# Decay table moved to the loads' queue, activation table first, and zero matmuls in the waits of the first three chunks

## The chip, the cores and the metric

The kernel runs on one core of a Trainium2 chip. The metric is the device time of one execution in microseconds (us). TensorE (PE) multiplies matrices and loads their stationary operand on a side path (PEld); VectorE (DVE), ScalarE (ACT) and GpSimd (POOL) work on elements; SyncE (SP) and ACT issue DMA transfers here, each on a queue of its own, and all transfers run on the core's 16 DMA engines. An engine takes its instructions in the order in which they stand in its program, and so does a queue.

## The reference

Three stages follow one another: attention with a decay, a gated MLP, and a second MLP with `h * cos(h)`. Only the first stage is touched by the change. Its core:

```python
for b in range(nb):                      # blocks of 64 positions
    qb, kb, vb = (q[:, :, sl], k[:, :, sl], v[:, :, sl])
    intra = np.einsum('bhic,bhjc->bhij', qb, kb) * Dmask[None]     # lam ** (i - j), 0 above the diagonal
    intra = np.einsum('bhij,bhjd->bhid', intra, vb)
    inter = np.einsum('bhid,bhde->bhie', qb * lam_pow[None], kv_state)
    out[:, :, sl] = intra + inter
    kb_dec = kb * rev_pow[None]
    kv_state = lam_block[None, :, None, None] * kv_state + np.einsum('bhsd,bhse->bhde', kb_dec, vb)
```

There are 2 batches, 8 heads, 768 positions and a head size of 64; the MLPs take 1536 tokens of 512, with inner sizes 1536 and 2048, weights in float64.

## The kernel before

The attention runs in 12 chunks of 128 positions (6 in each batch), all 8 heads at once, two heads side by side on the 128 partitions. For chunk g the steps are, each a function:

- `load_qkv` (L215) issues the loads of q, k and v, 256 KB each, on SP's queue, into 3, 3 and 5 buffers.
- `att_t` (L275) has TensorE transpose q (with `anti`, which also reverses it) and k (with `ident`), and ScalarE copy the results to `qt` and `kt` (L279).
- `att_scores` (L331) multiplies `kt` and `qt`; `att_mask` (L337) has VectorE multiply the scores with the decay table `dmask`, giving `at`.
- `att_kd` (L293) has GpSimd scale k with a column of `dmask`; `att_state` (L308) multiplies `kd` and v into the running state.
- `att_out` (L351, and L357 for the state's part) gives the chunk's output, which ScalarE and VectorE split into a high and a low half (L93, L94).

`dmask` (512 KB) is built at the start. `lam` is loaded, VectorE works out its powers in `down` (seven steps, L240), ScalarE's queue writes `down` to DRAM as `down_d` (L245, 8 KB), and reads it back with an overlapping access pattern into all partitions (L247). The read has to wait until the write has landed; both are instructions in ScalarE's program, and what stands behind them on ScalarE waits too. Behind them stand the load of the activation table (with a one-column `warm` activation, L511) and then the copies of `qt` and `kt`. `spread` (L255) brings the row of powers to all partitions with a small matmul (`lrow`).

The order of everything is written out by hand: `manual_schedule` records the program in the order in which the functions are called. The start of it is

```python
tables()                       # lam, q0 k0 q1 k1, powers, down_d, dmask, v0, q2 k2
load_qkv(1, "v"); load_qkv(3, "qk"); load_qkv(2, "v")
for _ in range(WARM):          # WARM = 10 matmuls of zeros, 512 columns, bf16
    nc.tensor.matmul(ps, zeros[:, 0:P], zeros, start=True, stop=True)
att_t(0); att_scores(0); spread()
att_t(1, "acc"); att_scores(1)
att_mask(0); att_kd(0); att_mask(1); att_kd(1)
```

and then a loop over g: `att_state(g)`, `att_kd(g + 2)`, `att_out(g)`, for g = 0 also `att_t(2)`, the loads of chunk g + 4 (v of g + 3), in most turns one 512 KB piece of MLP weights on SP's queue, `att_scores(g + 2)`, `att_mask(g + 2)`, `att_t(g + 3)`. From g = 6 on, the first matmuls of the gated MLP are mixed in; after the attention the MLPs run with TensorE busy nearly without a gap.

The load of k of chunk 3 takes the buffer of k of chunk 0, and so waits on SP's queue for `att_kd(0)`, which needs `dmask`.

Of the kernel before, what the change touches and what calls it, by code (L numbers as in the profile page):

```python
# [12 lines left out]
AF = mybir.ActivationFunctionType  # L13
# [19 lines left out]
WARM = 10  # L33
# [4 lines left out]
def kernel(  # L38
# [17 lines left out]
    nc = tc.nc  # L56
    B, H, S, D = q.shape
    P = 128
# [3 lines left out]
    C = P  # L62
# [24 lines left out]
    def bank(where):  # L87
        pool = ps_acc if where == "acc" else ps_mm
        return pool.tile([P, 512], F32, tag=where, name=where)
# [118 lines left out]
    def load_qkv(g, what="qkv"):  # L208
        if g >= NCH:
            return  # L210
        for nm in what:
            b, c = divmod(g, CPB)
            src, bufs = {"q": (q, 3), "k": (k, 3), "v": (v, 5)}[nm]
            t = att.tile([P, H, D], F32, tag=nm, name=nm, bufs=bufs)
            nc.sync.dma_start(t, src[b, :, c * C:(c + 1) * C, :].rearrange("h p d -> p h d"))  # L215
            qkv[g, nm] = t
# [5 lines left out]
    down = att.tile([H, 2 * C], F32, name="down", bufs=1)  # L222
    anti = att.tile([P, P], F32, name="anti", bufs=1)
    dmask = att.tile([P, H, C], F32, name="dmask", bufs=1)
    sel = att.tile([H, DM], F32, name="sel", bufs=1)
    lrow = att.tile([P, NPAIR, C], F32, name="lrow", bufs=1)
    state = [att.tile([P, NPAIR, P], F32, name=f"state{i}", bufs=1) for i in range(2)]

    def tables():

        nc.scalar.dma_start(down[:, C - 1:C], lam.rearrange("(h o) -> h o", o=1))
        load_qkv(0, "qk")
        load_qkv(1, "qk")
        nc.vector.memset(down[:, C + 1:], 0.0)
        nc.vector.memset(down[:, C:C + 1], 1.0)
        n = 1
        while n < C:
            nc.vector.tensor_scalar(  # L240
                out=down[:, C - 2 * n:C - n], in0=down[:, C - n:C],
                scalar1=down[:, C - n:C - n + 1], scalar2=None, op0=ALU.mult,
            )
            n *= 2
        nc.scalar.dma_start(down_d, down)  # L245
        e = down_d[:, :]
        nc.scalar.dma_start(dmask, bass.AP(e.tensor, e.offset + 1, [[1, P], [2 * C, H], [1, C]]))  # L247
        load_qkv(0, "v")
        load_qkv(2, "qk")

    def spread():

        ps = bank("acc")
        for p in range(NPAIR):
            nc.tensor.matmul(  # L255
                ps[:, p * C:(p + 1) * C], sel[:, p * P:(p + 1) * P], down[:, 0:C],
                start=True, stop=True,
            )
        nc.vector.tensor_copy(lrow.rearrange("p a i -> p (a i)"), ps)
# [7 lines left out]
            xs[nm, blk] = tuple(xp.tile([P, KD, TB], F32R, tag=t, name=t) for t in ("xh", "xl"))  # L267
        return xs[nm, blk]

    def att_t(g, where="mm"):  # L270

        for nm, src, perm in (("qt", qkv[g, "q"], anti), ("kt", qkv[g, "k"], ident)):
            ps = bank(where)
            for p in range(NPAIR):
                nc.tensor.transpose(  # L275
                    ps[:, p * P:(p + 1) * P], src[:, 2 * p:2 * p + 2, :].rearrange("p a d -> p (a d)"), perm
                )
            t = att.tile([P, NPAIR, C], F32, tag=nm, name=nm)
            nc.scalar.activation(t.rearrange("p a i -> p (a i)"), ps, AF.Copy)  # L279
            live[g, nm] = t  # L280
            if nm == "qt" and g % CPB:
                qd = att.tile([P, NPAIR, C], F32, tag="qd", name="qd", bufs=3)
                nc.vector.tensor_tensor(
                    out=qd[:, :, ::-1], in0=ps.rearrange("p (a i) -> p a i", a=NPAIR), in1=lrow, op=ALU.mult
                )
                live[g, "qd"] = qd
                tick()
# [33 lines left out]
                nc.vector.tensor_copy(new[r, :, r], pv[r])  # L321
        tick()

    def att_scores(g):
        qt, kt = live[g, "qt"], live[g, "kt"]
        got = live[g, "s"] = [bank("mm") for _ in range(2)]

        for p in range(NPAIR):
            for h2, ps in enumerate(got):
                r = slice(64 * h2, 64 * h2 + 64)  # L330
                nc.tensor.matmul(ps[:, p * C:(p + 1) * C], kt[r, p, :], qt[r, p, :], start=True, stop=True)  # L331
# [11 lines left out]
    def att_out(g):  # L343
        at, vn = live.pop((g, "at")), qkv[g, "v"]
        ps = bank("acc")
        inter = g % CPB != 0

        for p in range(NPAIR):
            cs = slice(p * C, (p + 1) * C)
            for h2 in range(2):  # L350
                nc.tensor.matmul(  # L351
                    ps[64 * h2:64 * h2 + 64, cs], vn[:, 2 * p + h2, :], at[:, 2 * p + h2, :],
                    start=p == 0, stop=not inter and p == NPAIR - 1, skip_group_check=True,
                )
        if inter:
            for p in range(NPAIR):
                nc.tensor.matmul(  # L357
                    ps[:, p * C:(p + 1) * C], state[g % 2][:, p, :], live[g, "qd"][:, p, :],
                    start=False, stop=p == NPAIR - 1, skip_group_check=True,
                )  # L360
        xh, xl = x_tiles(g // CB)
        o = (g % CB) * C
        split(xh[:, :, o:o + C], xl[:, :, o:o + C], ps.rearrange("p (a i) -> p a i", a=NPAIR))
# [129 lines left out]


    with tc.manual_schedule():
        nc.vector.memset(halfpi, math.pi / 2)
        zeros = att.tile([P, 512], mybir.dt.bfloat16, name="zeros", bufs=1)
        nc.vector.memset(zeros, 0.0)
        nc.gpsimd.memset(anti, 0.0)
        nc.gpsimd.affine_select(  # L500
            out=anti, in_=anti, compare_op=ALU.not_equal, fill=1.0, base=1 - P, pattern=[[1, P]], channel_multiplier=1
        )
        make_identity(nc, ident)
        nc.gpsimd.tensor_copy(
            sel.rearrange("k (h d) -> k h d", d=D), ident[0:H, 0:H].rearrange("k (h o) -> k h o", o=1).to_broadcast([H, H, D])
        )
        tables()
        load_qkv(1, "v")
        load_qkv(3, "qk")
        load_qkv(2, "v")  # L510
        nc.scalar.activation(warm, halfpi, AF.Silu)  # L511
        for t in state:
            nc.vector.memset(t, 0.0)

        ps = bank("acc")
        for _ in range(WARM):
            nc.tensor.matmul(ps, zeros[:, 0:P], zeros, start=True, stop=True)
        att_t(0)
        att_scores(0)
        spread()  # L520
        att_t(1, "acc")
        att_scores(1)
        att_mask(0)
        att_kd(0)
        att_mask(1)
        att_kd(1)
        for g in range(NCH):
            chunk[0] = g
            att_state(g)
            if g + 2 < NCH:  # L530
                att_kd(g + 2)
            att_out(g)
            if g == 0:
                att_t(2, "acc")
            load_qkv(g + 4, "qk")
            load_qkv(g + 3, "v")
            for _ in range(RAWS[g]):
                if n_loaded[0] - n_conv[0] + len(converting) < STAGE:
                    load_piece()
            if g + 2 < NCH:  # L540
                att_scores(g + 2)
                att_mask(g + 2)
            if g + 3 < NCH:
                att_t(g + 3)
            half = HALVES.index(g) if g in HALVES else -1
            if half >= 0:
                (produce_val if half % 2 else produce_gate)(half // 2, "acc")
                if half % 2:
                    finish(half // 2)()
        while converting:  # L550
            tick(age=0)
        flush()
        while n_loaded[0] - n_conv[0] < STAGE:
            load_piece()
        att_stack.close()
        mlp["sum"] = ctx.enter_context(tc.tile_pool(name="sum", bufs=NBLK))
        ring.append(ctx.enter_context(tc.tile_pool(name="ring_b", bufs=RING_B)))
        done = 0
        finished = len(HALVES) // 2
        convert(finished - 1, 0)  # L560
        for u in range(finished, NU):
            ph = units[u][0]
            low = []

            def finish_to(n):
                nonlocal finished
                while finished <= n:
                    low.append(finish(finished))
                    finished += 1

            produce(u)
            finish_to(u - ph)
            while done <= u - LAG:
                consume(done)
                done += 1
            convert(u, (2 if u < EASE else 1) if units[u][0] == 0 else u % 2)
            for fn in low:
                fn()
        while finished < NU:
            finish(finished)()  # L580
            finished += 1
        while done < NU:
            consume(done)
            done += 1
# [30 lines left out]
```

## Time and profile before

| | |
|---|---|
| Median of 3 runs | 632.95 us (631.49, 633.10, 632.95) |
| The profiled execution's own time | 632.53 us |
| Its span, first to last instruction | 630.5 us |
| PE busy | 619.2 us, 98% of the span |
| PE's share of the chain that ended last | 96% |
| ACT and DVE in that chain | 1% each |
| Mean granted TensorE clock | 0.989 of full |

The profile gives, for each engine, how long it was busy, in total and in slices of the span; the granted clock of TensorE; for each instruction its start, its length and what ended the engine's idle time before it; and the chain of work followed back from the last instruction. The time of an execution is longer than its span by what lies around it, here 632.53 − 630.5 = 2.03 us.

### The profile page before, as it was taken

To read this page: it belongs to the slowest core of one execution; us is meant where nothing else is said; L and a number is where in the kernel's file an instruction comes from. 1 tells how busy PE (TensorE), PEld (TensorE's weight loads), DVE (VectorE), ACT (ScalarE), POOL (GpSimd) and SP (SyncE) were. 2 spreads that over 40 slices of the span, in tenths; PEclk is the share of its full clock that TensorE was granted. 3 is DMA by queue.
4 is the path that set the end of the run, shared out by engine and by line. 5 is a ranking of instruction groups with operands and counts; after the bars stand their busy time and mean duration, and the time that the engine had idled before them with its cause. 6 is when DMAs were issued, how large, how long until landed. Compare 5 with 4: busy or idle time off the path is not lost.

```text
span 630.5 us, 8212 instructions
## 1 busy us (share of the span) xinstructions
PE 619.2 (98%) x3186; PEld 512.3 (81%) x3186; DVE 417.9 (66%) x632; ACT 272.0 (43%) x462; POOL 133.0 (21%) x115
## 2 busy tenths in 40 slices
PE   6999999999999999999999999999999999999997
PEld 4788888888888888888888888888888888888886
DVE  2677746778887613487514788897788678766655
ACT  1334334554334311334213465555555555544441
POOL 2224411333333200023203434101101010100000
PEclk7799999999999999999999999999999999999999
DMA  9998223444434200235200120212121110000103
GB/s 184 182 232 232 75 66 103 134 133 135 133 101 151 83 1 0 68 111 155 67 1 33 35 67 34 68 33 68 33 68 34 68 33 2 0 2 1 67 4 131
DMA packets 65431, 49.30 MB, mean 78 GB/s; under 512 B 38760, under 2 KB 60272, under 8 KB 65392
## 3 DMA queue, kind: packets, MB, share of 16 engines
q1 hardware_dynamic: 64320, 48.24, 27.1%
q10 hardware_dynamic: 1072, 0.53, 0.4%
q8 instruction: 25, 0.41, 0.3%
q14 instruction: 14, 0.11, 0.1%
HBM read 45.61 MB, written 3.15 MB: 77 GB/s over the span
## 4 chain that ended last, share of the span: by engine, by line
PE 96%; DVE 1%; ACT 1%; DMA 1%; issue 0%; ACTq 0%
PE mm L99 16%; PE mm L100 16%; PE mm L101 16%; PE acc L99 13%; PE acc L101 13%; PE acc L100 13%; PE mm L331 2%; PE acc L351 2%; PE acc L357 2%; PE mm L275 1%; PE acc L308 1%; DMA down_d<-down 1%; DVE sum L471 0%; PE acc L275 0%; ACT kt L279 0%; PE acc L255 0%
## 5 line engine op out<-in xcount | busy, mean ns | idle before, releaser
L99 PE MATMUL mm<-xl,wh 128*128 128x512 f32 x456 | 177.4, 389 | 0.0
L100 PE MATMUL mm<-xh,wl 128*128 128x512 f32 x456 | 177.4, 389 | 0.0
L101 PE MATMUL mm<-xh,wh 128*128 128x512 f32 x456 | 177.4, 389 | 0.0
L94 POOL TENSOR_TENSOR wl<-cw,wh 128x512 fp32r<-128x512 f32 x68 | 93.1, 1380 | 372.1 <-ACT wh L93 339.8
L433 DVE TENSOR_TENSOR g<-s,mm 128x512 f32<-128x512 f32 x81 | 55.4, 683 | 77.8 <-PE mm L101 75.5
L101 PEld LDWEIGHTS mm<-xh,wh 128*128 128x128 f32 x456 | 85.6, 188 | 17.8
L100 PEld LDWEIGHTS mm<-xh,wl 128*128 128x128 f32 x456 | 85.6, 188 | 17.7
L99 PEld LDWEIGHTS mm<-xl,wh 128*128 128x128 f32 x456 | 85.6, 188 | 17.7
L438 DVE TENSOR_TENSOR gl<-g,gh 128x512 fp32r<-128x512 f32 x84 | 68.1, 811 | 30.4 <-ACT gh L434 30.4
L434 ACT ACTIVATE gh<-g 128x512 fp32r<-128x512 f32 x84 | 52.3, 623 | 73.1 <-DVE g L433 73.1
L99 PE MATMUL acc<-wl,gh 128*128 128x512 f32 x192 | 74.7, 389 | 0.0
L100 PE MATMUL acc<-wh,gl 128*128 128x512 f32 x192 | 74.7, 389 | 0.0
L101 PE MATMUL acc<-wh,gh 128*128 128x512 f32 x192 | 74.7, 389 | 0.0
L144 ACT ACTIVATE ct<-raw 128x512 f32<-128x512 f32 x68 | 45.5, 670 | 65.6 <-DVE cw L161 38.3
L424 ACT ACTIVATE s<-s 128x512 f32<-128x512 f32 x48 | 30.4, 633 | 77.4 <-DVE s L423 77.4
L159 DVE TENSOR_SCALAR cw<-raw 128x512 int32<-128x512 int32 x68 | 49.5, 728 | 21.4 <-POOL wl L94 21.3
L422 DVE SCALAR_TENSOR_TENSOR s<-n,mm 128x512 f32<-128x512 int32 x48 | 32.9, 685 | 37.9 <-ACT n L421 37.7
L99 PE MATMUL acc<-gl,wh 128*128 128x512 f32 x144 | 56.0, 389 | 0.0
L100 PE MATMUL acc<-gh,wl 128*128 128x512 f32 x144 | 56.0, 389 | 0.0
L101 PE MATMUL acc<-gh,wh 128*128 128x512 f32 x144 | 56.0, 389 | 0.0
L161 DVE SCALAR_TENSOR_TENSOR cw<-ct,cw 128x512 int32<-128x512 int32 x68 | 49.0, 721 | 2.1
L165 DVE SCALAR_TENSOR_TENSOR cw<-raw,cw 128x512 int32<-128x512 int32 x68 | 48.0, 706 | 2.1
(75 smaller groups left out, 692.5 us busy)
## 6 DMA issues: line engine op xcount, KB each, us to landing
raw<-in_moe_w_out_dram SPq DMA_DIRECT2D x28, 512.0 KB, 3.3
raw<-in_moe_w_in_dram SPq DMA_DIRECT2D x16, 512.0 KB, 3.7
raw<-in_moe_w_gate_dram SPq DMA_DIRECT2D x12, 512.0 KB, 3.6
raw<-in_moe_w_val_dram SPq DMA_DIRECT2D x12, 512.0 KB, 3.7
q<-in_q_dram SPq DMA_DIRECT2D x12, 256.0 KB, 4.9
k<-in_k_dram SPq DMA_DIRECT2D x12, 256.0 KB, 4.8
v<-in_v_dram SPq DMA_DIRECT2D x12, 256.0 KB, 5.1
out_dram<-sum SPq DMA_DIRECT2D x12, 256.0 KB, 2.0
```

Of the source, the lines that this page charges most:

```text
L94: (sub or nc.vector).tensor_tensor(out=lo, in0=src, in1=hi.bitcast(F32), op=ALU.subtract)
L99: nc.tensor.matmul(ps, wh, xl, start=first, stop=False)
L100: nc.tensor.matmul(ps, wl, xh, start=False, stop=False)
L101: nc.tensor.matmul(ps, wh, xh, start=False, stop=last)
L144: nc.scalar.activation(t, words[:, :, 1].bitcast(F32), AF.Copy, scale=2.0 ** -112)
L159: nc.vector.tensor_scalar(out=w, in0=lo, scalar1=29, scalar2=None, op0=ALU.logical_shift_right)
L161: nc.vector.scalar_tensor_tensor(out=w, in0=t.bitcast(I32), scalar=3, in1=w, op0=ALU.logical_shift_left, op1=ALU.bitwise_or)
L165: nc.vector.scalar_tensor_tensor(out=w, in0=hi, scalar=-0x80000000, in1=w, op0=ALU.bitwise_and, op1=ALU.bitwise_or)
L422: nc.vector.scalar_tensor_tensor(out=s, in0=n_, scalar=-TWO_PI_1, in1=up, op0=ALU.mult, op1=ALU.add)
L433: nc.vector.tensor_tensor(out=g, in0=s, in1=up, op=ALU.mult)
L434: nc.scalar.activation(gh, g, AF.Copy)
L438: nc.vector.tensor_tensor(out=gl, in0=g, in1=gh.bitcast(F32), op=ALU.subtract)
```

## The change

The read of `dmask` moves from ScalarE's queue to SP's, behind the loads of q, k of chunks 0 and 1 and v of chunk 0, which in turn moves ahead of q and k of chunk 2. The activation table is loaded before the write of `down_d`. `spread` goes ahead of `att_scores(0)`. TensorE gets 15 more matmuls of zeros beside the ten that it had, each 512 columns in bf16: 2 ahead of `att_t(1)`, 4 ahead of `att_scores(1)`, 3 ahead of `att_out(0)`, 2 ahead of `att_t(2)` and 4 ahead of `att_scores(2)`. They write the PSUM bank that the step behind them then overwrites. The memset of `zeros` becomes VectorE's first instruction.

```diff
@@ -222,6 +222,7 @@
     down = att.tile([H, 2 * C], F32, name="down", bufs=1)
     anti = att.tile([P, P], F32, name="anti", bufs=1)
     dmask = att.tile([P, H, C], F32, name="dmask", bufs=1)
+    zeros = att.tile([P, 512], mybir.dt.bfloat16, name="zeros", bufs=1)
     sel = att.tile([H, DM], F32, name="sel", bufs=1)
     lrow = att.tile([P, NPAIR, C], F32, name="lrow", bufs=1)
     state = [att.tile([P, NPAIR, P], F32, name=f"state{i}", bufs=1) for i in range(2)]
@@ -231,8 +232,10 @@
 
 
         nc.scalar.dma_start(down[:, C - 1:C], lam.rearrange("(h o) -> h o", o=1))
+        nc.scalar.activation(warm, halfpi, AF.Silu)
         load_qkv(0, "qk")
         load_qkv(1, "qk")
+        load_qkv(0, "v")
         nc.vector.memset(down[:, C + 1:], 0.0)
         nc.vector.memset(down[:, C:C + 1], 1.0)
         n = 1
@@ -244,8 +247,7 @@
             n *= 2
         nc.scalar.dma_start(down_d, down)
         e = down_d[:, :]
-        nc.scalar.dma_start(dmask, bass.AP(e.tensor, e.offset + 1, [[1, P], [2 * C, H], [1, C]]))
-        load_qkv(0, "v")
+        nc.sync.dma_start(dmask, bass.AP(e.tensor, e.offset + 1, [[1, P], [2 * C, H], [1, C]]))
         load_qkv(2, "qk")
 
     def spread():
@@ -267,10 +269,16 @@
             xs[nm, blk] = tuple(xp.tile([P, KD, TB], F32R, tag=t, name=t) for t in ("xh", "xl"))
         return xs[nm, blk]
 
-    def att_t(g, where="mm"):
+    def zero(ps, n):
+        for _ in range(n):
+            nc.tensor.matmul(ps, zeros[:, 0:P], zeros, start=True, stop=True)
+
+    def att_t(g, where="mm", idle=0):
 
         for nm, src, perm in (("qt", qkv[g, "q"], anti), ("kt", qkv[g, "k"], ident)):
             ps = bank(where)
+            if nm == "qt":
+                zero(ps, idle)
             for p in range(NPAIR):
                 nc.tensor.transpose(
                     ps[:, p * P:(p + 1) * P], src[:, 2 * p:2 * p + 2, :].rearrange("p a d -> p (a d)"), perm
@@ -321,9 +329,10 @@
                 nc.vector.tensor_copy(new[r, :, r], pv[r])
         tick()
 
-    def att_scores(g):
+    def att_scores(g, idle=0):
         qt, kt = live[g, "qt"], live[g, "kt"]
         got = live[g, "s"] = [bank("mm") for _ in range(2)]
+        zero(got[0], idle)
 
         for p in range(NPAIR):
             for h2, ps in enumerate(got):
@@ -343,6 +352,8 @@
     def att_out(g):
         at, vn = live.pop((g, "at")), qkv[g, "v"]
         ps = bank("acc")
+        if g == 0:
+            zero(ps, 3)
         inter = g % CPB != 0
 
         for p in range(NPAIR):
@@ -493,9 +504,8 @@
 
 
     with tc.manual_schedule():
+        nc.vector.memset(zeros, 0.0)
         nc.vector.memset(halfpi, math.pi / 2)
-        zeros = att.tile([P, 512], mybir.dt.bfloat16, name="zeros", bufs=1)
-        nc.vector.memset(zeros, 0.0)
         nc.gpsimd.memset(anti, 0.0)
         nc.gpsimd.affine_select(
             out=anti, in_=anti, compare_op=ALU.not_equal, fill=1.0, base=1 - P, pattern=[[1, P]], channel_multiplier=1
@@ -508,18 +518,14 @@
         load_qkv(1, "v")
         load_qkv(3, "qk")
         load_qkv(2, "v")
-        nc.scalar.activation(warm, halfpi, AF.Silu)
         for t in state:
             nc.vector.memset(t, 0.0)
 
-        ps = bank("acc")
-        for _ in range(WARM):
-            nc.tensor.matmul(ps, zeros[:, 0:P], zeros, start=True, stop=True)
-        att_t(0)
+        att_t(0, idle=WARM)
+        spread()
         att_scores(0)
-        spread()
-        att_t(1, "acc")
-        att_scores(1)
+        att_t(1, "acc", idle=2)
+        att_scores(1, idle=4)
         att_mask(0)
         att_kd(0)
         att_mask(1)
@@ -531,14 +537,14 @@
                 att_kd(g + 2)
             att_out(g)
             if g == 0:
-                att_t(2, "acc")
+                att_t(2, "acc", idle=2)
             load_qkv(g + 4, "qk")
             load_qkv(g + 3, "v")
             for _ in range(RAWS[g]):
                 if n_loaded[0] - n_conv[0] + len(converting) < STAGE:
                     load_piece()
             if g + 2 < NCH:
-                att_scores(g + 2)
+                att_scores(g + 2, idle=0 if g else 4)
                 att_mask(g + 2)
             if g + 3 < NCH:
                 att_t(g + 3)
```

On SP's queue, at the start of the program (q, k, v are the chunks' loads, in the order q0 k0 q1 k1 v0, then `dmask`, then q2 k2 v1 q3; the names in brackets are semaphores that a row waits for):

```order
 L215 DMA k<-in_k_dram 128x8x64
 L215 DMA v<-in_v_dram 128x8x64
+L250 DMA dmask<-down_d 128x8x128 [waits DMAHW4_49]
 L215 DMA q<-in_q_dram 128x8x64 [waits DMAHW0_49]
 L215 DMA k<-in_k_dram 128x8x64 [waits DMAHW1_49]
 L215 DMA v<-in_v_dram 128x8x64 [waits DMAHW2_49]
```

The new row waits for the write of `down_d`, and the loads of chunk 2, v of chunk 1 and all later loads stand behind it.

On ScalarE, at the start of the program, before the change:

```order
L233 DMA down<-in_lam_dram 8x1
L245 DMA down_d<-down 8x256 [waits DMAHW0_49,DVE_49]
L247 DMA dmask<-down_d 128x8x128 [waits DMAHW4_49]
L511 ACT_TABLE_LOAD
L511 ACTIVATE warm<-halfpi 128x1
L279 ACTIVATE qt<-mm 128x512 [waits PE_49]
```

and after it:

```order
L234 DMA down<-in_lam_dram 8x1
L235 ACT_TABLE_LOAD
L235 ACTIVATE warm<-halfpi 128x1 [waits DVE_49]
L248 DMA down_d<-down 8x256 [waits DMAHW0_49,DVE_49]
L287 ACTIVATE qt<-mm 128x512 [waits PE_49]
```

Between the write of `down_d` and the first copy of `qt` nothing is left on ScalarE.

On TensorE, from the first transposes to the output of chunk 0, before the change:

```order
L275 MATMUL mm<-anti,q 128x128 x4
L275 MATMUL mm<-ident,k 128x128 x4
L331 MATMUL mm<-qt,kt 128x128 x8
L255 MATMUL acc<-down,sel 128x128 x4
L275 MATMUL acc<-anti,q 128x128 x4
L275 MATMUL acc<-ident,k 128x128 x4
```

and after it (a pair of rows with `zeros` is one matmul of zeros and its weights):

```order
L283 MATMUL mm<-ident,k 128x128 x4
L257 MATMUL acc<-down,sel 128x128 x4
L340 MATMUL mm<-qt,kt 128x128 x8
L274 LDWEIGHTS zeros
L274 MATMUL acc<-zeros 128x512
...
L283 MATMUL acc<-anti,q 128x128 x4
L283 MATMUL acc<-ident,k 128x128 x4
L274 LDWEIGHTS zeros
L274 MATMUL mm<-zeros 128x512
...
L340 MATMUL mm<-qt,kt 128x128 x8
L316 MATMUL acc<-v,kd 64x64 x8
```

The small matmul of `spread` now stands between the transposes and the scores of chunk 0, and zeros stand ahead of the steps of chunk 1.

## Rows read from the trace of the kernel before

**Rows 1.** Page, part 2: 40 equal slices, PE busy and granted clock in tenths.

```profile
PE   6999999999999999999999999999999999999997
PEclk7799999999999999999999999999999999999999
```

**Rows 2.** Windows: stretch, length, busy us (instructions) PE, PEld, DVE, ACT, POOL; PEclk, DMA share, GB/s.

```profile
4.00:6.00 2.00, 2.00 (x9) 1.08 (x8) 0.94 (x2) 0.00 (x0) 0.00 (x0) 1.00 1.25 219
...
8.00:10.00 2.00, 0.00 (x0) 0.00 (x0) 0.00 (x0) 1.81 (x3) 0.00 (x0) 0.71 1.35 218
...
20.00:22.00 2.00, 2.00 (x26) 1.79 (x22) 1.51 (x4) 0.00 (x0) 1.36 (x2) 0.50 1.08 180
22.00:24.00 2.00, 1.38 (x10) 1.02 (x8) 1.02 (x2) 1.56 (x3) 0.88 (x2) 0.88 0.00 0
```

**Rows 3.** Timeline, TensorE, to 29 us: start, length, line, tiles, count, [idle before <-releaser].

```profile
1.22 4.40 PE L517 MATMUL acc<-zeros 128*128 128x512 bf16 x10 [1.22 <-DVE zeros L498]
5.45 0.60 PE L275 MATMUL mm<-anti,q 128*128 128x128 f32 x4
...
10.70 2.08 PE L331 MATMUL mm<-qt,kt 64*128 64x128 f32 x16 [4.21 <-ACT kt L279]
12.71 2.07 PE L255 MATMUL acc<-down,sel 8*128 8x128 f32 x8
14.71 1.11 PE L275 MATMUL acc<-anti,q 128*128 128x128 f32 x4
...
17.36 2.08 PE L331 MATMUL mm<-qt,kt 64*128 64x128 f32 x16 [0.69 <-ACT kt L279]
19.37 1.12 PE L308 MATMUL acc<-v,kd 128*64 128x64 f32 x16
20.28 1.92 PE L351 MATMUL acc<-at,v 128*64 128x128 f32 x16
22.13 0.81 PE L275 MATMUL acc<-anti,q 128*128 128x128 f32 x4
...
24.18 1.16 PE L331 MATMUL mm<-qt,kt 64*128 64x128 f32 x16 [0.80 <-ACT kt L279]
...
28.87 1.16 PE L331 MATMUL mm<-qt,kt 64*128 64x128 f32 x16
```

**Rows 4.** Timeline, the same stretch: DMA issues (SPq, ACTq), ScalarE and GpSimd.

```profile
3.87 1.14 SPq L215 DMA_DIRECT2D v<-in_v_dram  x1
3.95 0.29 ACTq L245 DMA_DIRECT2D down_d<-down  x1
...
7.75 0.40 ACTq L247 DMA_DIRECT2D dmask<-down_d  x1
8.18 1.28 ACT L511 ACT_TABLE_LOAD   x1 [8.18 <-DMA down_d<-down]
...
13.51 2.07 POOL L293 TENSOR_TENSOR kd<-k,dmask 128x512 f32<-128x512 f32 x2 [11.03 <-DMA dmask<-down_d]
14.59 0.37 SPq L215 DMA_DIRECT2D k<-in_k_dram  x1
```

**Rows 5.** Chain of work that ended last, in order of time: start, length, engine, tile, line.

```profile
25.34 1.02 PE mm L275 x8
26.36 0.62 PE acc L308 x16
26.98 0.88 PE acc L351 x16
...
53.78 0.23 PE acc L99
```

**Rows 6.** DMA issues by line: queue, count, KB each, median us from issue to landing.

```profile
raw<-in_moe_w_out_dram SPq DMA_DIRECT2D x28, 512.0 KB, 3.3
...
raw<-in_moe_w_val_dram SPq DMA_DIRECT2D x12, 512.0 KB, 3.7
...
dmask<-down_d ACTq DMA_DIRECT2D x1, 512.0 KB, 5.6
```

## The prediction

> **What bounds the kernel now.** Read the slices first [rows 1]: TensorE is at nine tenths or more in all but the first and the last slice, and its granted clock is full in all but the first two. So after some 25 us nothing but less matmul work could shorten the kernel, and the change takes none of that away. What it can win lies in the first 24 us, and what it wins there moves everything behind it forward, as long as no load becomes late.
>
> Next, the stretch itself, window by window [rows 2], and TensorE's timeline over it [rows 3]. TensorE works from 1.22 to about 6.5 (ten matmuls of zeros, then the transposes of chunk 0), stands still for 4.21 us until ScalarE has copied `kt`, and from 10.70 works nearly without a gap. But the clock has fallen in the gap: 0.71 of full in 8 to 10 us, 0.50 in 20 to 22, 0.88 in 22 to 24. That is the lower level, 1.2 GHz, from just under 9 us to about 22.5. The durations say the same: the scores take 2.08 us until then and 1.16 us from 24.18 on [rows 3]. One trap: the column reads 1.00 in 4 to 6 us [rows 2], yet the ten zeros go out 0.42 us apart ((5.45 − 1.22) / 10), where a matmul of 512 columns takes 0.23 us later [rows 3, 5]. They ran at the lower level; the clock rose about when they ended.
>
> Why ScalarE is late: its program holds the issue of the `dmask` read, which waits for the write of `down_d`; that write goes out at 3.95 and lands at 7.75, then the table load takes 1.28 us, and only then `qt` and `kt` are copied [rows 4]. `dmask` lands 5.6 us after its issue [rows 6]; GpSimd starts `kd` at 13.51, and the load of k of chunk 3 follows at 14.59 [rows 4].
>
> **The change part by part.** *ScalarE.* The table load (1.28 us) moves into the time between the load of `lam` and 3.95, where ScalarE only waits for VectorE; the issue of `dmask` goes to SP. With both gone `qt` and `kt` of chunk 0 are copied as soon as the transposes end, at about 7.2. Were the table load to slip past 3.95, it would delay `down_d` by that much; a start after `lam`'s issue leaves it about a microsecond.
>
> *`dmask` on SP.* It waits for the same write, so I issue it at 7.75 again, behind v of chunk 0, whose issue ends at 5.01 [rows 4]. Two bounds on its landing: 5.6 us, as before, when it shared the engines with four loads; and 3.3 us, the shortest row of a transfer of its size [rows 6]. I take 4.0, nearer the lower one, because by about 8 us the five loads ahead of it are through (5 × 0.262 MB at about 220 GB/s [rows 2], 6 us from the first data at about 2) and SP issues nothing else while it waits; not 3.3, since those transfers have longer rows. So `dmask` lands at 11.75 (11.05 to 13.35) instead of 13.35. The Trainium skill, "DMA: Bandwidth & Descriptors", section "Queues, rings and completion order", says that an engine takes turns between queues: on ScalarE's queue `dmask` had turns of its own, which it gives up. Here nothing stands before it, so by that page it would get the double share, land about 3.5 us after its issue, and the sum below would be 625.4. No row of before shows it on SP.
>
> *TensorE, clock held.* With no 4 us gap I let the clock stay at its upper level after the zeros. Then: transposes 1.02 us (1.96 at the lower level, 14.71 to 16.67) to 6.5; `spread` 1.0, half of its 2.0; scores 1.1; two zeros 0.46; transposes of chunk 1 to 10.1; four zeros 0.92; scores of chunk 1 to 12.1 [rows 3, 5]. Now `dmask` is last: `kd` starts 0.16 us after the landing, as before (13.51 − 13.35), at 11.9, and half of 2.07 is 1.04, so chunk 0's state can start at 12.95. State 0.62, three zeros 0.69, output 0.88, two zeros 0.46, transposes of chunk 2 1.02, four zeros 0.92 [rows 5]: 4.59 us. VectorE's masks run from 11.9 to 13.2 and are hidden behind state and zeros; the copy of `kt` (0.8 us after the transposes, the idle of that row) behind the last four zeros, nearly to the end. Scores of chunk 2 start at 17.54, where they started at 24.18 [rows 3]. **Gain 6.65 us.** The 15 zeros cost 3.5 us on TensorE at the upper level; where the wait is longer than they are they cost nothing, and behind the landing of `dmask` some 2 us of them (those before output and transposes) lie on the path. I count that in full.
>
> *Bounds.* `dmask` at 13.35: gain 5.05. `dmask` at 10.9 or earlier: TensorE's own 12.1 binds, and the gain grows by 12.95 − 12.1 to 7.5.
>
> *What queues behind.* On SP q, k of chunk 2, v of 1 and q of 3 now wait for `dmask`. After 11.75 each takes 0.262 MB / 220 GB/s = 1.19 us: k of 2 lands at 14.1, needed at 16.1; k of 3, issued after `kd` at 12.95, lands behind them at about 17.7, needed about 19.1. The slack is small but there; later chunks take 4.69 us each (28.87 − 24.18 [rows 3]) for three loads of 1.19. That VectorE clears `zeros` first moves TensorE's start by about 0.1 us, hidden behind `dmask`.
>
> **Sum.** The profiled execution took 632.53 us; 632.53 − 6.65 = 625.9. It lies 0.4 below the median 632.95, which would give 626.3. I take 626.1. Its own range: 632.53 − 7.5 = 625.0 to 632.95 − 5.05 = 627.9.
>
> **Rivals.**
>
> *The clock rises late.* Ten zeros were just enough in this execution, and the transposes and `spread` that follow ran at the lower level for 2 us each at 12.71 and 14.71 without raising it [rows 3]. If the clock has not risen by 5.4, all goes at half speed until zeros and scores lift it: scores of chunk 0 end at 11.5, zeros 12.3, transposes 14.3, zeros 16.0. Risen at 12.3, scores of chunk 2 start at 19.9 (gain 4.2, 628.3); at 16.0, at 21.7 (gain 2.5, 630.0); at 18.05, at 22.65 (gain 1.5, 631.0). For it: the rise falls where the zeros end, with nothing to spare. Against: the same ten zeros did lift it. The Trainium skill, "TensorE: Matmul & The Clock Gate", section "What's actually happening", says that the number of slow matmuls before the rise differs between runs of one kernel, 6, 11 or 14. By it ten are sometimes too few; the one trace here shows ten. The middle of this case is 629.6.
>
> *Zeros at half speed: slower.* If the clock stays low all the way, the zeros are on the path at 0.43 us each: 16.0 as above, scores 18.05, state and output 2.76 (22.13 − 19.37) with three zeros 1.29 to 22.1, zeros 0.86, transposes 1.96, zeros 1.72: scores of chunk 2 at 26.6, 2.4 us later than now, 634.9 to 635.4. It decides from the point where the clock is still low when chunk 0's output starts. Against: the scores, state and output of chunk 1 and 0 alone raised it by 22.5 before [rows 2, 3].
>
> *Loads late.* If the loads behind `dmask` need 1.6 us each instead of 1.19, k of chunk 3 lands at 19.75, 0.65 late, and chunks that also load a 512 KB weight piece fall further behind: up to 2 us lost, 628.1. For: DMA engines go empty from about 8 us until `dmask` flows. Against: the slack above.
>
> *`dmask` no sooner.* The move does not do what it says, the read takes 5.6 us wherever it stands: 627.5 to 627.9.
>
> **How the numbers follow.** Chances: forecast 0.58, late clock 0.21, loads late 0.10, `dmask` no sooner 0.04, slower 0.07. A measurement of this kernel tells a change from none at about 0.3%, 1.9 us: faster means below 631.05. All of the forecast, loads late and `dmask` no sooner are faster, and two thirds of the late clock (0.14); its last third (0.07) is the same. So faster 0.86, same 0.07, slower 0.07. The range runs from 624.7 (0.3 below the forecast's own end, for a noise of the runs) to 630.4, which takes in all of the first three and two thirds of the late clock: 0.86, less what the forecast's edges lose.
>
> **What would show it.** Clock 1.00 in every window from 6 to 24 us; `qt` of chunk 0 copied near 6 to 7; `kd` starting near 11.9; scores of chunk 2 near 17.5; the MLP shifted by as much. Half-speed scores (2.08 us) after 8 us speak for a late clock; idle TensorE ahead of the transposes of chunk 2 or 3, ended by a load, for loads late; `kd` at 13.5 for the last rival. I am wrong if the attention starts earlier and the MLP does not, for then something behind 24 us gives the gain back.

## The result and the profile after

| | before | after |
|---|---|---|
| Median | 632.71 us (4 runs, 631.49 to 633.10) | 625.96 us (4 runs, 625.60 to 626.03) |
| Profiled execution, its own time | 632.53 us | 625.91 us |
| Its span | 630.5 us | 624.1 us |
| Mean granted TensorE clock | 0.989 | 1.0 |

The changed kernel is faster; the ratio is 0.9895, with a 95% interval of 0.9878 to 0.9913. The forecast was 626.1 us in a range of 624.7 to 630.4. The executions also lie closer together than before. One execution of all the runs below, of 690.03 us at a mean clock of 0.851, is left out of the comparisons.

The windows of the changed kernel (columns as in [rows 2]) answer the rows that showed the fallen clock:

```profile
6.00:8.00 2.00, 2.00 (x25) 1.87 (x24) 0.69 (x1) 0.71 (x2) 0.00 (x0) 1.00 1.22 201
8.00:10.00 2.00, 2.00 (x19) 1.44 (x16) 0.10 (x1) 0.73 (x2) 0.00 (x0) 1.00 0.36 103
10.00:12.00 2.00, 1.62 (x19) 1.00 (x17) 0.74 (x2) 0.35 (x1) 0.03 (x1) 1.00 1.07 276
12.00:14.00 2.00, 0.92 (x18) 0.74 (x19) 2.00 (x4) 0.00 (x0) 2.00 (x2) 1.00 1.34 236
...
20.00:22.00 2.00, 2.00 (x37) 1.83 (x37) 1.66 (x4) 0.68 (x2) 1.30 (x2) 1.00 1.01 227
```

The granted clock is 1.00 in every one. The column alone would not prove a full clock, since it can read 1.00 over slow matmuls (the run with four zeros, below, shows this); the durations in the timeline prove it. TensorE's idle stretch has shrunk to part of 10 to 14 us. From 8 to 10 us the DMA engines moved 103 GB/s, less than half of what they moved before [rows 2]; the kernel before had such holes later, with 61 GB/s from 14 to 16 us and none moved from 22 to 24. In finer slices (0.175 us each, from 6 to 13 us) the hole is

```profile
GB/s 215 221 227 215 214 236 227 227 219 176 100 38 0 0 0 0 0 0 108 190 304 304 293 307 272 287 287 284 237 259 266 263 275 293 286 287 271 246 230 219
```

SP had nothing behind v of chunk 0 to issue while it waited for the write of `down_d`, so the engines ran dry at about 8.1 us, and the table, issued at 8.02, brought its first data at about 9.1. The hole returns below.

The timeline of the changed kernel (start, length, line, tiles, count, idle before and releaser), against [rows 3] and [rows 4]:

```profile
1.19 3.87 PE L274 MATMUL mm<-zeros 128*128 128x512 bf16 x10 [1.19 <-DVE halfpi L508]
...
4.89 0.60 PE L283 MATMUL mm<-anti,q 128*128 128x128 f32 x4
...
5.53 0.60 ACT L287 ACTIVATE qt<-mm 128x512 f32<-128x512 f32 x1 [2.66 <-PE mm L283]
...
7.09 1.16 PE L340 MATMUL mm<-qt,kt 64*128 64x128 f32 x16
...
11.97 2.07 POOL L301 TENSOR_TENSOR kd<-k,dmask 128x512 f32<-128x512 f32 x2 [9.49 <-DMA dmask<-down_d]
13.05 1.01 SPq L215 DMA_DIRECT2D k<-in_k_dram  x1
13.08 0.69 PE L316 MATMUL acc<-v,kd 128*64 128x64 f32 x16 [1.46 <-POOL kd L301]
...
17.75 1.16 PE L340 MATMUL mm<-qt,kt 64*128 64x128 f32 x16
...
19.34 0.60 PE L283 MATMUL mm<-ident,k 128*128 128x128 f32 x4
...
22.45 1.16 PE L340 MATMUL mm<-qt,kt 64*128 64x128 f32 x16
```

The copy of `qt` follows the transposes at once; the scores of chunk 0 start at 7.09 instead of 10.70 and take 1.16 us instead of 2.08; the only wait of TensorE that counts is the 1.46 us for `kd`, which waits for the table. The scores of chunk 2 start at 17.75 instead of 24.18, 6.43 us earlier. From there on the chunks keep their period (22.45 − 17.75 = 4.70 us), and the chain of work shows the path behind the table (start, length, engine, tile, line):

```profile
3.92 4.09 DMA down_d<-down
8.02 3.80 DMA dmask<-down_d
11.97 1.07 POOL kd L301
13.08 0.69 PE acc L316 x16
13.76 0.75 PE acc L274 x3
14.52 1.02 PE acc L362 x16
15.54 0.54 PE acc L274 x2
16.08 0.87 PE acc L283 x8
16.95 0.86 PE mm L274 x4
17.82 1.10 PE mm L340 x16
...
618.37 2.73 DVE sum L482 x4
```

It starts with two transfers, the write of the powers and the read of the table, and then runs on TensorE to the end. The zeros (L274) stand in it three times. The last sums of the kernel before began at 624.80 us, by the same view of its trace:

```profile
624.80 2.73 DVE sum L471 x4
```

Now they begin at 618.37: again 6.43 us, so nothing behind the attention gave any of it back.

### The profile page after: what moved, and what is told of

Same layout as the page of the kernel before. It is cut to its first block, busy times and chain, and to the rows that moved or that the text cites. A ratio compares the mean times of both kernels' runs of the same rounds, so it can differ in the third digit from the quotient of the medians.

```text
span 624.1 us, 8240 instructions
## 1 busy us (share of the span) xinstructions
PE 617.0 (99%) x3201; PEld 509.1 (82%) x3201; DVE 417.9 (67%) x632; ACT 272.2 (44%) x462; POOL 133.0 (21%) x115
## 4 chain that ended last, share of the span: by engine, by line
PE 96%; DMA 1%; DVE 1%; issue 0%; ACT 0%; POOL 0%; POOLq 0%
PE mm L99 17%; PE mm L100 17%; PE mm L101 17%; PE acc L99 13%; PE acc L101 13%; PE acc L100 13%; PE acc L362 2%; PE mm L340 2%; PE acc L368 2%; PE mm L283 1%; PE acc L316 1%; DMA down_d<-down 1%; DMA dmask<-down_d 1%; DVE sum L482 0%; DVE down L243 0%
## 5 line engine op out<-in xcount | busy, mean ns | idle before, releaser
L100 PEld LDWEIGHTS mm<-xh,wl 128*128 128x128 f32 x456 | 85.6, 188 | 17.7
```

Source lines behind the costliest of these rows:

```text
L100: nc.tensor.matmul(ps, wl, xh, start=False, stop=False)
```

## The experiments

Medians of the kernel before beside these runs were 632.2 to 632.6 us. The changed kernel, run again beside the first group and beside the last:

> The changed kernel once more, unaltered, as the yardstick for the runs beside it. Every theory expects about 626.0 us, 6.7 us under the kernel before, with the granted clock at 1.00 from 6 to 24 us and the scores of chunk 2 starting near 17.7.

> The changed kernel once more, unaltered, as the yardstick on this chip: about 626.0 us.

Measured: 625.93 us (625.79 to 626.05), and 625.83 us (625.49 to 626.01). This is the yardstick for what follows. The second of three groups (q of chunk 2 ahead of the table with the early zeros only, the zeros alone, the activation table late, four zeros at the start) ran on a chip on which only the kernel before was run beside it, so for these four a difference of a few tenths of a us proves nothing.

### Are the added zeros needed?

```diff
-        if g == 0:
-            zero(ps, 3)
...
-        att_t(1, "acc", idle=2)
-        att_scores(1, idle=4)
+        att_t(1, "acc")
+        att_scores(1)
...
-                att_t(2, "acc", idle=2)
+                att_t(2, "acc")
...
-                att_scores(g + 2, idle=0 if g else 4)
+                att_scores(g + 2)
```

> The changed kernel without its 15 added matmuls of zeros; the ten at the start stay. Theory 1, the zeros hold the clock: TensorE then idles about 0.8 us ahead of the scores of chunk 1 and about 2 us ahead of the state of chunk 0, the clock falls to the lower level near 12 us, state, output, transposes and scores behind it run at half speed, and the time is 628 to 630. Theory 2, the zeros are not needed: the clock stays at 1.00, the zeros on the path behind the landing of the decay table (three and two at about 0.22 us, the last four hidden behind the copy of kt) go away, and the time is about 1.1 us under the changed kernel, 624.9.

Measured: 626.10 us (625.74 to 626.97), within 0.2 us of the changed kernel. Neither theory gave this number, and the profiled execution shows why (windows, then timeline):

```profile
12.00:14.00 2.00, 1.08 (x25) 0.89 (x24) 2.00 (x4) 0.00 (x0) 1.96 (x2) 0.90 1.34 226
14.00:16.00 2.00, 2.00 (x18) 1.67 (x15) 1.15 (x3) 0.34 (x1) 1.64 (x3) 0.50 1.39 224
16.00:18.00 2.00, 1.34 (x8) 1.10 (x6) 1.29 (x2) 1.42 (x3) 0.71 (x2) 0.74 1.20 203
```

```profile
11.07 1.16 PE L340 MATMUL mm<-qt,kt 64*128 64x128 f32 x16 [0.74 <-ACT kt L287]
...
13.15 0.77 PE L316 MATMUL acc<-v,kd 128*64 128x64 f32 x16 [0.92 <-POOL kd L301]
13.69 1.93 PE L360 MATMUL acc<-at,v 128*64 128x128 f32 x16
...
18.09 1.16 PE L340 MATMUL mm<-qt,kt 64*128 64x128 f32 x16 [0.75 <-ACT kt L287]
```

The clock did fall, as theory 1 says, near 13.6 us and for about 3.5 us: the output took 1.93 us instead of 1.09. But the zeros that are no longer on the path pay for it: the scores of chunk 2 start at 18.09, 0.34 us later than in the changed kernel. Of the four executions two had a mean clock of 0.997 (626.24 and 626.97 us) and two of 0.999 to 1.0 (625.74 and 625.97 us); by this the fall does not come each time, though only one of the four has a trace. What the zeros buy is steadiness, not time: they cost nearly as much as the slow stretch that they prevent. Even the two executions whose clock held did not reach the 624.9 of theory 2; the next run shows a reason.

Keeping only the six zeros ahead of the table's landing:

```diff
-        if g == 0:
-            zero(ps, 3)
...
-                att_t(2, "acc", idle=2)
+                att_t(2, "acc")
...
-                att_scores(g + 2, idle=0 if g else 4)
+                att_scores(g + 2)
```

> The changed kernel with the zeros of chunk 1 (two and four, ahead of its transposes and scores) and without the nine behind the landing of the decay table (three, two and four). Theory 1, zeros hold the clock: those that stay do it, since they fill the wait ahead of the table; clock at 1.00 and 624.9, the 1.1 us of zeros on the path gone. Theory 2, no zeros are needed: the same 624.9, and so the same as without any. If the late nine are what holds the clock: lower level from about 14 us and 628 to 630.

Measured: 625.83 us (625.62 to 626.13), a mean clock of 1.00 in all four: here the nine late zeros were not what held it. But the 1.1 us did not come. Timeline:

```profile
16.60 1.16 PE L340 MATMUL mm<-qt,kt 64*128 64x128 f32 x16 [0.80 <-ACT kt L287]
17.69 0.66 PE L283 MATMUL mm<-anti,q 128*128 128x128 f32 x4
19.04 0.63 PE L283 MATMUL mm<-ident,k 128*128 128x128 f32 x4 [0.69 <-DMA k<-in_k_dram]
...
22.17 1.16 PE L340 MATMUL mm<-qt,kt 64*128 64x128 f32 x16
```

The scores of chunk 2 start at 16.60, 1.15 us earlier than in the changed kernel, just as expected. Then TensorE waits for k of chunk 3, which lands at about 18.9. The chain of work that ended last runs through this load:

```profile
13.19 5.71 DMA k<-in_k_dram
```

By the scores of chunk 3 only 0.28 us are left (22.17 against 22.45). The gain was given back one step later, to a load.

### The load that is next

q of chunk 2 into the hole ahead of the table, with the early zeros only:

```diff
         load_qkv(0, "v")
+        load_qkv(2, "q")
...
-        load_qkv(2, "qk")
+        load_qkv(2, "k")
```

> The changed kernel with the six zeros of chunk 1 only, and q of chunk 2 loaded ahead of the decay table instead of behind it. Theory A, formed from the run without the late zeros: k of chunk 3 lands at about 19.0 whatever TensorE does, because SP issues nothing from about 5 us to the issue of the table and the DMA engines run dry, and this load now sets the pace. One more load in that hole takes 1.19 us from the queue behind the table: the table lands no later (kd near 12.0), k of chunk 3 lands near 17.9, the 0.7 us wait ahead of its transposes is gone, the scores of chunk 3 start near 21.3 and the time is 624.9. Theory B, something else holds chunk 3 up, or the table is pushed back by the load ahead of it: 625.8 to 626.8.

Measured: 624.77 us (624.69, 624.73, 624.77, 625.28, and one of 626.79 at a mean clock of 0.997). Timeline and window of its profiled execution:

```profile
8.00:10.00 2.00, 2.00 (x26) 1.69 (x23) 0.47 (x1) 0.16 (x1) 0.00 (x0) 1.00 1.21 238
```

```profile
12.11 3.09 POOL L302 TENSOR_TENSOR kd<-k,dmask 128x512 f32<-128x512 f32 x3 [9.63 <-DMA dmask<-down_d]
...
18.19 0.60 PE L284 MATMUL mm<-ident,k 128*128 128x128 f32 x4
...
21.30 1.16 PE L341 MATMUL mm<-qt,kt 64*128 64x128 f32 x16
```

The hole is gone (238 GB/s, where the changed kernel moved 103 and the run without the late zeros 124), the wait ahead of the second transposes is gone, and the scores of chunk 3 start at 21.30, where theory A put them. The profiled executions of these two runs differ by 0.85 us, and the last sums of their traces by 0.84 (617.23 against 618.07). With these zeros one execution in five still lost the clock, by its mean. The same load moved with all zeros kept:

> The changed kernel with all its zeros, and q of chunk 2 loaded ahead of the decay table. It completes a square of two edits (late zeros kept or not, this load behind or ahead). Theory A, two limits stand side by side, the late zeros on TensorE and the landing of k of chunk 3, and taking away one leaves the other: here the zeros bind, scores of chunk 2 start near 17.7, and the time is 625.9, the same as the changed kernel. Theory B, the load alone was the limit: 624.8.

Measured: 626.35, 626.47 and 626.51 us; no trace of these three was taken. So the load by itself wins nothing, and even costs some 0.6 us (625.49 to 626.01 for the changed kernel on the same chip), which theory A did not expect. A table that lands later behind one more load would cost as much: it landed at 12.03 us in the trace of the run before and at 12.39 in that of the run below, both with this load ahead, against 11.73 to 11.96 without it. That this is the cause is not shown. The square is: neither edit 625.9, late zeros away 625.8, load ahead 626.5, both 624.8. Two limits lay side by side; each hides what the other is worth.

The zeros moved into the two waits that are left, with the load ahead (edit beside that of the load; the three ahead of the output and the two ahead of the transposes are taken away, as above):

```diff
     def att_state(g):
...
         ps = bank("acc")
+        if g == 0:
+            zero(ps, 4)
...
-                att_scores(g + 2, idle=0 if g else 4)
+                att_scores(g + 2, idle=0 if g else 3)
```

> q of chunk 2 ahead of the decay table, and the late zeros put where TensorE waits anyway: four (0.86 us) ahead of the state of chunk 0, in the wait of 1.0 us for kd, and three (0.65 us) ahead of the scores of chunk 2, in the wait of 0.8 us for kt; none ahead of the output or the transposes. If zeros cost nothing in a wait that is longer than they are and everything elsewhere, scores of chunk 2 start near 16.6 and the time is 624.8, with no execution in which the clock falls (without these zeros one of five went to 626.8 at a mean clock of 0.997). If they cost wherever they stand: 625.5 to 626.3.

Measured: 625.32 us (624.84 to 625.69), no execution below a clock of 1.0. In the profiled one the table landed later, `kd` starting at 12.47 and the scores of chunk 2 at 16.96 behind a last wait of 0.15 us: the zeros in the waits cost nothing there (4.49 us from `kd` to these scores, as in the run with the early zeros only), and the time follows the table's landing. By its median this version lies 0.5 us below the changed kernel on the same chip, but the two ranges overlap. Of the five executions with the load ahead and the early zeros only, four (624.69 to 625.28) lie below every execution of the changed kernel and the fifth (626.79) above them all. These runs do not decide between the two versions.

### Which move carried the gain?

The table's read on ScalarE's queue again, but behind the copies of chunk 0, so that it blocks none of them:

```diff
-        nc.sync.dma_start(dmask, bass.AP(e.tensor, e.offset + 1, [[1, P], [2 * C, H], [1, C]]))
...
         att_t(0, idle=WARM)
+        e = down_d[:, :]
+        nc.scalar.dma_start(dmask, bass.AP(e.tensor, e.offset + 1, [[1, P], [2 * C, H], [1, C]]))
```

> The changed kernel with the read of the decay table issued from ScalarE's queue again, but behind the copies of qt and kt of chunk 0, so that it holds up neither of them and shares the engines with the loads of chunk 2 and after as before. Theory 1, the table lands sooner because it has the engines alone: here it takes 5.6 us again (3.8 behind the loads), GpSimd starts kd at about 13.8 instead of 12.0, and the time is 1.8 us above the changed kernel, 627.8. Theory 2, the queue does not matter and the gain comes from ScalarE and the clock alone: kd near 12 and 626.0.

Measured: 629.03 us median; two of six executions took 627.87 and 628.00 at a mean clock of 0.999, four 628.65 to 629.68 at 0.996 to 0.997. Timeline of the first:

```profile
7.79 0.40 ACTq L524 DMA_DIRECT2D dmask<-down_d  x1
...
13.69 3.09 POOL L299 TENSOR_TENSOR kd<-k,dmask 128x512 f32<-128x512 f32 x3 [11.21 <-DMA dmask<-down_d]
14.80 0.69 PE L314 MATMUL acc<-v,kd 128*64 128x64 f32 x16 [2.37 <-POOL kd L299]
```

Theory 1 holds: issued at about the same time as in the kernel before, among the loads of chunks 1 to 3, the table again lets `kd` start only at 13.7, and the time is 1.9 us above the changed kernel where the clock holds. What was not expected is that the longer wait (2.37 us instead of 1.46) seems to cost the clock in most executions, 0.8 to 1.8 us more; no trace of those was taken, so that is read from their mean clock alone. So where the clock holds, of the 6.3 us (632.24 − 625.93) some 4.4 come with everything but the table's earlier landing, and 1.9 with that landing, which also keeps the wait short. In the median of the six executions the first part is only 3.2 us. That it is ScalarE being free that carries it is told by the runs on the other parts: the zeros and the activation table's place are worth little by themselves (below). The new places of `spread` and of v of chunk 0 were not tried apart.

The zeros alone, on the kernel before (loads, table and `spread` at their old places):

> The kernel before with the 15 zeros and nothing else: the table's read and the activation table stand on ScalarE as before. Theory 1, zeros help only where TensorE would otherwise wait a short time: the 4 us wait for kt stands ahead of all of them, the clock falls near 9 us, and the zeros run on the path at half speed: 633 to 635, slower than before by 1 to 3. The rival, that the zeros by themselves keep the clock and carry a good part of the gain: 628 to 630.

Measured: 632.74 us (10 runs), ratio 1.0008 (0.9999 to 1.0017): no difference. Slower than before was the right direction at most by 0.4 us; the expected 1 to 3 us did not come. Windows:

```profile
8.00:10.00 2.00, 0.00 (x0) 0.00 (x0) 0.00 (x0) 1.57 (x3) 0.00 (x0) 1.00 1.35 218
10.00:12.00 2.00, 1.06 (x10) 1.06 (x12) 0.00 (x0) 0.89 (x2) 0.00 (x0) 0.75 1.27 255
...
16.00:18.00 2.00, 2.00 (x10) 1.63 (x9) 0.54 (x1) 0.91 (x2) 0.11 (x1) 0.54 0.91 208
18.00:20.00 2.00, 2.00 (x30) 1.38 (x29) 1.56 (x4) 0.28 (x1) 0.00 (x0) 1.00 1.17 220
```

The clock falls at about 11.0 us, at the end of TensorE's wait of 4.94 us for `kt`, later than the near 9 us expected, and is back by 18 us instead of 22.5 [rows 2]. The scores of chunk 2 start at 24.36 against 24.18 before: what the earlier rise saves, the 15 zeros cost. Zeros behind a long wait carry none of the gain.

The activation table's load at its old place in the program, behind the write of `down_d`:

```diff
-        nc.scalar.activation(warm, halfpi, AF.Silu)
...
         load_qkv(2, "v")
+        nc.scalar.activation(warm, halfpi, AF.Silu)
```

> The changed kernel with the activation table's load at its old place in the program, behind the write of the powers' table to DRAM, but with the decay table's read on SP. Theory 1: the table's load is worth nothing by itself, since it now follows the issue of that write at about 4.2 us and ends near 5.5, before the transposes of chunk 0 do in most executions: 626.0. The rival, that putting it first carries part of the 4 us: qt of chunk 0 is copied more than 1 us later and the time is 626.5 to 627.3.

Measured: 626.17 us (625.96 to 626.57), ratio 0.9907 (0.9894 to 0.9921). ScalarE's timeline:

```profile
4.21 1.28 ACT L520 ACT_TABLE_LOAD   x1 [4.21 <-DVE down L242]
...
5.92 0.60 ACT L286 ACTIVATE qt<-mm 128x512 f32<-128x512 f32 x1 [0.21 <-PE mm L282]
```

The load ends before `qt` is due. Putting it first is worth at most some 0.3 us (626.17 against the yardstick's 625.83 and 625.93), by the spread of the runs and the change of chip not to be told from nothing; it was in the way only while it stood behind the issue of the table's read, which waits for `down_d` to land.

The rival of a late clock, priced by four zeros at the start instead of ten:

```diff
-WARM = 10
+WARM = 4
```

> The changed kernel with four matmuls of zeros at the start instead of ten: the clock is not lifted before the transposes of chunk 0. It prices the rival of a late clock. If that rival's arithmetic holds, scores of chunk 0 take 2.08 us, the clock rises only among the zeros and scores of chunk 1 at 13 to 17 us, and the time is 628 to 631. If the wait for the decay table hides the slow start, since TensorE waits there until 13.0 anyway, the scores of chunk 1 may end up to 1 us late and the time is 626.0 to 627.5.

Measured: 627.51 us (627.40 to 627.73). Timeline:

```profile
6.37 2.07 PE L257 MATMUL acc<-down,sel 8*128 8x128 f32 x8
8.37 2.08 PE L340 MATMUL mm<-qt,kt 64*128 64x128 f32 x16
...
11.21 0.93 PE L283 MATMUL acc<-anti,q 128*128 128x128 f32 x4
11.98 0.60 PE L283 MATMUL acc<-ident,k 128*128 128x128 f32 x4
...
14.46 0.69 PE L316 MATMUL acc<-v,kd 128*64 128x64 f32 x16
...
19.14 1.16 PE L340 MATMUL mm<-qt,kt 64*128 64x128 f32 x16
```

The durations fall from the lower level's to the upper level's in the transposes at 11.2 to 12.0. The granted clock's column does not show the slow stretch: over `spread` and the scores, at 2.07 and 2.08 us, it reads

```profile
8.00:10.00 2.00, 2.00 (x17) 1.78 (x17) 0.69 (x1) 0.00 (x0) 0.00 (x0) 1.00 0.36 110
```

The state of chunk 0 starts at 14.46 with no wait for `kd` left, 1.38 us later than in the changed kernel (13.08); TensorE itself is 2.84 us later (14.46 against 10.46 + 1.16 = 11.62), and the wait of 1.46 us absorbs the rest. So a clock that rises at 11 to 12 us costs 1.6 us here, at the upper end of what the second expectation allowed. A later rise was not seen and is not priced by this run.

## Why the prediction was right

The path was the forecast one: the write, the table, `kd`, then TensorE with its late zeros to the end. It won 6.43 us where 6.65 was forecast.

*ScalarE.* Right. `qt` at 5.53 and `kt` 0.6 later, expected by 7.2. The table's load slipped past nothing.

*The table's landing.* 3.80 us after its issue (4.0 taken, 3.3 and 5.6 the bounds). The issue came at 8.02 instead of 7.75, because `down_d` took 4.09 us to land instead of 3.80. The two errors, 0.27 late and 0.20 short, nearly cancel, so that `kd` started at 11.97 where 11.9 was forecast; that it came so close is in part luck. It is not luck alone: in six profiles with this order of transfers on SP the write took 3.71 to 4.09 us and the table 3.80 to 4.28, the longer one with the shorter other, and together 7.82 to 8.04 (3.71 + 4.23 and 4.09 + 3.80, for example). Why is open. The estimate by the turns between queues, which the Trainium skill, "DMA: Bandwidth & Descriptors", "Queues, rings and completion order", describes, was 3.5 us, 0.3 short. The run on ScalarE's own queue, where `kd` started at 13.69, agrees with such turns, but does not tell them from another way of sharing the engines.

*TensorE behind it.* 4.67 us measured from the state to the scores of chunk 2 (17.75 − 13.08), 4.59 forecast. Counting the late zeros in full was right for this kernel. What the forecast did not see is that without them nothing would be won: k of chunk 3 would have set nearly the same pace.

*The loads.* This step was mis-sized. I had k of chunk 3 land at 17.7 with a slack of 1.4 us; in the changed kernel it lands at about 19.0, 5.9 us after its issue at 13.05, and TensorE takes it at 19.34, so that the slack was 0.4. The loads ahead of it kept the forecast's pace of 1.19 us each to about 0.3 us (k of chunk 2, v of 1 and q of 3 landed at 14.4, 15.6 and 16.8, forecast 14.1, 15.3 and 16.5); the last step took 2.2 us instead. v of chunk 2 and q of chunk 4, issued behind it, landed at 19.8 and 19.7, so the three came in nearly together; why is open. The rival "loads late", with 1.6 us a load, was closer to deciding than its 0.10 says (1.4 us a load measured, from the table's landing at 11.82). It did not decide, because the zeros delay the need.

*The clock.* It was at its upper level from the transposes at 4.89 on, as the durations show. The rise came among the ten zeros or right behind them: in the changed kernel's three profiles these take 3.70 us (4.89 − 1.19), 3.57 and 4.24, where ten slow ones take 4.23 [rows 3]. The Trainium skill, "TensorE: Matmul & The Clock Gate", "What's actually happening", says that the number of slow matmuls before the rise differs between runs of one kernel, and these runs agree. In the profiles without the added zeros and without the late ones all ten zeros and the first transposes at 5.43 were slow (1.06 us): there the condition of the rival "the clock rises late", not risen by 5.4, was met. But `spread`, right behind these transposes, took 1.15 us and not 2.07, so the clock had risen by about 7 us, and `kd` at 12.04 and 12.11 was no later than elsewhere. So the rival went wrong in its next step, that nothing ahead of the zeros and scores of chunk 1 would lift the clock. Its prices are not refuted. They already count that TensorE would else wait for the table (12.3 + 1.02 + 0.92 + 1.1 = 15.3, past the state's 12.95), and the run with four zeros bears out the lowest: there `spread` starts at 6.37 (7.4 in the rival's sum), the clock rises at 11.2 to 12.0 (12.3), and the scores of chunk 2 start at 19.14 (19.9).

*Slower.* Half-speed zeros all the way did not occur: with four zeros at the start the clock rose in the transposes of chunk 1, by 12 us, and in the kernel before with the 15 zeros by 18 us.

## What to carry to other kernels

A queue's wait stops all that stands behind it on the issuing engine (here ScalarE's table load stood until 8.18 behind a write issued at 3.95), so put a transfer that must wait for another on an engine whose program has nothing due, and give its queue enough to do ahead of the wait. Matmuls of zeros are free only in a wait that is longer than they are; behind the last arrival they stand on the path. How many are needed these runs do not settle: by the mean clock, with waits of 0.7 to 1.0 us on TensorE, it held in two of four executions without added zeros and in eight of nine with six. When an edit that should gain gives nothing, look one step further: here two limits of about the same size, zeros and a load, hid each other until both were moved.

## What was not expected of the hardware

- A write of 8 KB to DRAM takes 3.5 to 4.1 us to land while five or six loads of 256 KB are in flight; it is the longest piece ahead of the table. Where it landed sooner the table took longer: the table's landing moved only between 11.73 and 11.96 us in six profiles.
- The granted clock's column reads 1.00 over the first zeros in every profile, while ten of them need 3.6 to 4.2 us, and with four zeros it reads 1.00 up to 12 us over matmuls at the lower level; until the column has changed for the first time the durations are the better witness.
- A load of 256 KB lands up to 6.1 us after its issue when the queue ahead of it is full (k of chunk 3, 5.9 to 6.1 us in the changed kernel's three profiles), although 0.262 MB are 1.2 us of the measured 220 GB/s.
